# Retention and two gated layers: first two weight units in quarters, weight steps by tables, product order at the ends

## Chip, core and metric

The kernel runs on one core of a Trainium2 chip. The metric is device time in microseconds (us). Its engines, as the profile names them: TensorE (PE; PEld are its weight loads), VectorE (DVE), ScalarE (ACT), GpSimd (POOL) and SyncE (SP), which issues most of the loads.

## The reference

Attention with decay (retention) over 2 batches, 8 heads, 768 positions and head size 64, then two feed-forward layers over its 1536 rows of 512:

```python
state = gamma[None, :, None, None] * state + np.einsum('bhd,bhe->bhde', k[:, :, t], v[:, :, t])
y[:, :, t] = scale * np.einsum('bhd,bhde->bhe', q[:, :, t], state)
...
x = (x @ w_a) * (x @ w_b) @ w_out          # 512 -> 1536 -> 512
h = x @ w_in                               # 512 -> 2048
x = (h * (1.0 / (1.0 + np.exp(-1.702 * h)))) @ w_out
```

## The kernel before

**Retention.** Twelve blocks `n` of 128 positions. Each has on PE scores (`ps_sc`), the state update (`ps_kv`, not for the last block of a sequence), and `ps_av` from the masked scores `a` and from the state; scores of block n+1 are issued at the start of block n. DVE masks the scores (L207), POOL scales q and v, ACT copies the state and casts results. Inputs come as `qv` and `kk`, 512 KB each (`kk` of a sequence's last block 256 KB), four buffers each: a load waits until the block four before has let its buffer go.

**Numbers.** Matmuls run on pairs of high and low parts (`a1h`, `a1l` and so on): ACT casts the high part, DVE subtracts for the low one (L66). The layers' products use a scheme with seven products in place of eight: each *job* (12 in layer 1, 8 in layer 2) has products named 1 to 7, of 12 matmuls each. Products 1, 2, 3 use direct weights `wd`, the others sums of them, `wt`. Product (j, i) is product i of job j. Behind product 1, ACT copies its bank x into bank y (L648), on which 6, 5 and 3 go on; behind 6 and 5 it copies y to `u` (L654, L656). 7 and 4 build a set w, which takes a bank of the same pool as x. Results are added or multiplied into `g` on DVE (L72, L75) or POOL.

**Weights** are stored in 64 bits and converted on the chip, in *units* of 1 MiB (`wraw`, two buffers): load (SP, two halves); *carry* (two ACT operations, L403 and L404); *bits* (two DVE, L409, L410), *sign* (DVE, L416), *add* (DVE, L422: adds what the low words carry). Then the `wd` cast on ACT (L434) and its low part on DVE, four *sums* on DVE (`tt`), and the `wt` cast and low part. `w_stream` is a generator of these steps; each `w_step` takes one, and `w_need` takes steps until the weights wanted are there.

**Order.** All engines run in the order in which the code is written. In retention, `EARLY_STEPS` says which steps of units 0 and 1 stand in which block; units 0 and 1 are loaded whole at the end of blocks 2 and 6 (`W_LOADS`). In `up`, behind each product one function of the list `later` (left-over splits of the retention results, or of layer 2's input sums `s12`, `s34`) or one weight step is taken, in layer 2 one of each. `down` multiplies with `w_out`: blocks of four 128-wide chunks of `g` (split to `ghl`), four quarters q each; `tick` takes one weight step behind each product there. Behind layer 1's down stage its sums become layer 2's operands.

Of the kernel before, what the change touches and what calls it, by code (L numbers as in the profile page):

```python
# [40 lines left out]
def retention_moe_kernel(  # L41
# [324 lines left out]
    wraw, wt, wtt = {}, {}, {}  # L366
    whl, w_half = {}, {}
    nxt = {"dma": 0}
    w_pools = {"d": [[wd, 2]], "t": []}
    w_where = {}  # L370
    more = {}
# [1 line left out]
    def w_room(kind):  # L373
        return sum(p[1] for p in w_pools[kind])

    def w_dma():
        i = nxt["dma"]
        if i >= len(units):
            return
        nxt["dma"] += 1  # L380
        what, ph, *rest = units[i]
        w = w1 if ph == 1 else w2
        t = rawp.tile([P, W, 2], I32, tag="wraw", name="wraw", bufs=2)
        v = t.rearrange("p a b -> p (a b)")
        if what == "d":
            for k, f in enumerate(rest):
                nc.sync.dma_start(out=v[:, k * W:k * W + W], in_=w[f][:, 3 - ph, :].bitcast(I32))
        else:

            p, m = rest  # L390
            nc.sync.dma_start(out=v[:, DM:DM + W], in_=w[2 * p][:, m, :].bitcast(I32))
            nc.sync.dma_start(
                out=v.rearrange("p (a b) -> p a b", a=4)[:, 0:4:3],
                in_=w[2 * p + 1][:, m, :].bitcast(I32).rearrange("p (a b) -> p a b", a=2),
            )
        wraw[i] = t
# [35 lines left out]
    def w_hi(kind, key, src):  # L432
        t = w_tile(kind, key)
        nc.scalar.copy(t[:, 0, 0:src.shape[-1]], src)  # L434
        w_half[kind, key] = t
# [34 lines left out]
        at = DM * (d_unit(f).index(f[1], 1) - 1)  # L470
        return whl["t", d_unit(f)][:, part, at:at + DM]

    EARLY = 1
    EARLY_STEPS = {5: [("carry", 0)], 6: [("bits", 0)], 7: [("sign", 0)], 8: [("add", 0)], 9: [("d", 0)], 10: [("sums", 0), ("carry", 1)], 12: [("second", 0)]}
    W_LOADS, LATER = (2, 6), (9,11)

    def w_stream():

        for i, u in enumerate(units):
            if i < EARLY:  # L480
                continue
            w_bits(i)
            yield
            w_sign(i)
            yield
            w_add(i)
            yield
            if u[0] == "j":
                while not w_room("d"):
                    yield  # L490
                w_hi(*w_direct(i))
                w_sums(i)
                yield
                w_lo(*w_direct(i))
                while not w_room("t"):
                    yield
                w_hi(*w_second(i))
                w_carry(i + 1)
                yield
                w_lo(*w_second(i))  # L500
                wt.pop(i)
                wtt.pop(i)
                yield
            else:
                while not w_room("t"):
                    yield
                it = "t", u[1:], wt.pop(i)
                w_hi(*it)
                w_carry(i + 1)
                yield  # L510
                w_lo(*it)
                yield
# [13 lines left out]

    POOL_LO = {}

    def w_early(n):

        for step, i in EARLY_STEPS.get(n, ()):
            if step == "sums":
                w_sums(i)
            elif step == "second":
                w_hi(*w_second(i))
                w_lo(*w_second(i))
                wt.pop(i)
                wtt.pop(i)
            elif step == "d":
                w_hi(*w_direct(i))  # L540
                w_lo(*w_direct(i))
            else:
                {"carry": w_carry, "bits": w_bits, "sign": w_sign, "add": w_add}[step](i)

# [5 lines left out]
    def retention_done():  # L550

        retention.close()
        kw = dict(reuse_waits="tile")
# [26 lines left out]
    class Job:  # L580
# [54 lines left out]
        def step(self, i):  # L635
# [34 lines left out]
                    return [(self.ph, 2 * self.p), (self.ph, 2 * self.p + 1)]  # L670
            return []

    def up_order(ph, n):
        if ph == 1:
            yield from ((0, 1), (0, 2), (0, 6), (0, 5), (0, 7), (0, 3), (1, 1), (0, 4), (1, 6), (1, 2), (1, 5))
        else:
            yield from ((0, 1), (1, 1), (0, 2), (1, 2), (0, 6), (1, 6), (0, 5), (1, 5), (0, 7), (0, 3), (2, 1), (0, 4))
            yield from ((2, 2), (1, 7), (2, 6), (1, 3), (2, 5), (1, 4))
# [3 lines left out]
        yield from ((j, 1), (j - 1, 7), (j, 2), (j - 1, 3), (j, 6), (j - 1, 4), (j, 5), (j, 7), (j, 3), (j, 4))  # L682

    ghl = {}
    saved = {}
# [35 lines left out]
    def up(ph):  # L721
        jobs = [Job(k) for k in jobs_of(ph)]
        n = len(jobs)
        n_chunks = (C1, C2)[ph - 1]
        order = [*up_order(ph, n)]
        todo = []
        for at, (j, i) in enumerate(order):
            ready = jobs[j].step(i)
            finish()
            for _ in range(2 if ph == 1 and 0 < at < 3 else 1):  # L730
                if later:
                    later.pop(0)()
            if not later or ph == 2:
                w_step()
            for f in todo:
                g_save(f)
            todo = [f for f in ready if f[1] < n_chunks - 6]
            if j == n - 1:

                room["big"] += {2: 2, 5: 2, 3: 2, 4: 1}.get(i, 0)  # L740
                g_next(ph, 4)
        assert not todo and not later

    def down(ph):
# [136 lines left out]
    with tc.manual_schedule():  # L881
        for t in state:
            nc.vector.memset(t, 0.0)
        att_constants()
        for n in range(RAWBUFS):
            att_load(n, "qv")
            att_load(n, "kk")
        ps = ps_att.tile([P, NP, P], F32, tag="av", name="ps_warm", bufs=3)
        warm(ps, WARM)
        att_v(0)  # L890
        att_load(RAWBUFS, "qv")
        att_vdec([1])
        nc.vector.tensor_scalar(
            out=causal, in0=causal, scalar1=0.0, scalar2=1.0, op0=ALU.is_gt, op1=ALU.mult
        )
        att_scores(0)
        att_q(1)
        att_qdec(2)
        warm(ps, 8, WARM)
        for n in range(NBLK):  # L900
            if n > 0:
                att_scores(n + 1)
            att_s_hi(n - 2)
            if n == 0:
                att_v(1)
                att_q(2)
                att_vdec(range(2, SEQ))
            else:
                att_q(n + 2)
                att_v(n + 1)  # L910
            att_load(n + 1 + RAWBUFS, "qv")
            att_kv(n)
            att_x_vector(n - 1)
            att_s_lo(n - 2)
            att_load(n + RAWBUFS, "kk")
            if n == 0:
                att_qdec(0)
            for c in ((3,), (4, 5))[n] if n < 2 else ():
                att_qdec(c)
            w_early(n)  # L920
# [6 lines left out]
            if n in W_LOADS:  # L927
                w_dma()
            if n in LATER:
                later.pop(0)()  # L930
# [11 lines left out]
        later[:0] = [lambda: (w_early(NBLK), att_s_hi(NBLK - 1), att_s_lo(NBLK - 1))]  # L942
        layer(1)
        layer(2)

# [65 lines left out]
```

## Time and profile before

| | |
|---|---|
| median of 3 runs (lowest, highest) | 608.9 us (608.0, 609.19) |
| profiled execution: time, span | 611.0 us, 609.2 us |
| mean granted clock of PE | 0.988 of 2.4 GHz |
| PE busy | 579.2 us, 95% |
| DVE, ACT, POOL busy | 420.9, 295.9, 66.0 us |
| DMA | 76.9 MB, 126 GB/s in the mean |

Busy shares are means over stages. Where time can go shows in the idle time of PE and in what released it: a row of the timeline carries in brackets the idle time before an instruction and its releaser.

### The profile page before, as it was taken

Reading aid. Unit: us, or ns where it says so; the run is one execution under the profiler, and the core shown is the slowest. Engines: PE = TensorE matmul, PEld = TensorE weight load, DVE = VectorE, ACT = ScalarE, POOL = GpSimd, SP = SyncE. Lnnn points to the kernel's source line nnn. Section 1 sums busy time; section 2 is a strip of 40 time slices with the busy share of each in tenths; the row PEclk is TensorE's granted clock in tenths of the full one; section 3 lists DMA queues with packets and bytes.
Section 4 is the critical chain, followed back from the end, with each engine's and each line's share of the span. In section 5 each row is a group of like instructions: output and inputs, shape, how many; then the busy total and the mean of one; then the engine's idle time right before and its main releaser. Section 6 shows DMA issues by size and latency. Waiting matters only on the chain.

```text
span 609.2 us, 8443 instructions
## 1 busy us (share of the span) xinstructions
PE 579.2 (95%) x3448; PEld 528.7 (87%) x3448; DVE 420.9 (69%) x478; ACT 295.9 (49%) x366; POOL 66.0 (11%) x145
## 2 busy tenths in 40 slices
PE   8979789999999999899999988999999999999997
PEld 8868679999999999788887877999998888888885
DVE  3669968788878866656688797776645646776422
ACT  3746543654554647337133475676658547070100
POOL 6844002030302030200000000000000000000000
PEclk9979989999999999999999998999999999999999
DMA  8982023424262222351503002564422443430022
GB/s 310 308 318 92 12 90 106 173 76 168 74 238 70 69 70 70 114 231 57 185 21 118 1 24 83 214 265 175 173 70 69 170 176 130 165 118 39 0 104 104
DMA packets 24263, 76.90 MB, mean 126 GB/s; under 512 B 2336, under 2 KB 2464, under 8 KB 24224
## 3 DMA queue, kind: packets, MB, share of 16 engines
q1 hardware_dynamic: 23648, 75.77, 35.2%
q8 instruction: 27, 0.44, 0.3%
q10 hardware_dynamic: 576, 0.59, 0.3%
q14 instruction: 12, 0.10, 0.1%
HBM read 60.62 MB, written 15.73 MB: 125 GB/s over the span
## 4 chain that ended last, share of the span: by engine, by line
PE 75%; DVE 14%; ACT 4%; DMA 4%; issue 3%; POOL 0%; ACTq 0%; DVEq 0%
PE ps L605 36%; PE ps L835 34%; DMA kk<-in_att_dram 3%; PE ps_sc L198 2%; DVE tt L69 2%; DVE wt L422 1%; DVE sum L72 1%; PE ps_av L244 1%; DVE wt L416 1%; DVE s34l L66 1%; DVE sum L69 1%; PE ps_kv L226 1%; ACT wraw L404 1%; ACT wt L403 1%; DMA causal<-in_cmask_dram 1%
## 5 line engine op out<-in xcount | busy, mean ns | idle before, releaser
L835 PE MATMUL ps<-wt,ghl 128*128 128x512 f32 x576 | 131.1, 389 | 0.8 <-DVE sum L72 0.8
L835 PEld LDWEIGHTS ps<-wt,ghl 128*128 128x128 f32 x576 | 108.0, 188 | 23.6 <-DVE sum L72 1.2
L835 PE MATMUL ps<-ghl,wt 128*128 128x512 f32 x432 | 98.7, 390 | 2.7 <-DVE g L75 2.1
L835 PEld LDWEIGHTS ps<-ghl,wt 128*128 128x128 f32 x432 | 80.9, 188 | 20.2 <-DVE g L75 2.6
L605 PE MATMUL ps<-a1h,wd 128*128 128x384 f32 x320 | 89.2, 341 | 7.8 <-DVE wd L66 3.0
L605 PE MATMUL ps<-s12h,wt 128*128 128x384 f32 x320 | 87.4, 335 | 1.0 <-ACT u L654 1.0
L66 DVE TENSOR_TENSOR ghl<-g,ghl 128x1536 fp32r<-128x1536 f32 x28 | 50.8, 1816 | 48.0 <-ACT ghl L272 47.9
L272 ACT CAST ghl<-g 128x1536 fp32r<-128x1536 f32 x28 | 41.0, 1481 | 58.1 <-PE ps L835 50.6
L605 PEld LDWEIGHTS ps<-a1h,wd 128*128 128x128 f32 x320 | 59.3, 192 | 10.0 <-DVE wd L66 4.0
L72 DVE TENSOR_TENSOR sum<-ps,sum 128x512 f32<-128x512 f32 (+1 forms) x41 | 36.9, 932 | 39.7 <-PE ps L835 39.6
L605 PEld LDWEIGHTS ps<-s12h,wt 128*128 128x128 f32 x320 | 58.3, 188 | 1.6 <-ACT u L654 1.4
L605 PE MATMUL ps<-s12l,wt 128*128 128x384 f32 x160 | 53.7, 336 | 1.5 <-DVE s12l L66 1.5
L605 PE MATMUL ps<-a1l,wd 128*128 128x384 f32 x160 | 54.2, 339 | 0.0
L72 DVE TENSOR_TENSOR u<-ps,u 128x768 f32<-128x768 f32 x28 | 26.8, 956 | 33.8 <-PE ps L605 32.1
L605 PE MATMUL ps<-s34h,wd 128*128 128x384 f32 x160 | 45.2, 344 | 3.1 <-ACT u L656 2.1
L75 POOL TENSOR_TENSOR g<-g,u 128x768 f32<-128x768 f32 x12 | 29.2, 2431 | 172.5 <-DVE u L72 113.3
L605 PE MATMUL ps<-a,wt 128*128 128x384 f32 x240 | 44.8, 334 | 0.0
L422 DVE CUSTOM_DVE_ANT_0 wt<-wraw,wt 128x2048 uint16<-128x2048 uint16 x34 | 43.3, 1273 | 1.4
L605 PE MATMUL ps<-s34h,wt 128*128 128x384 f32 x160 | 43.8, 334 | 0.0
L416 DVE SCALAR_TENSOR_TENSOR wt<-wraw,wt 128x1024 int32<-128x1024 int32 x34 | 41.5, 1221 | 0.6
L605 PEld LDWEIGHTS ps<-a,wt 128*128 128x128 f32 x240 | 41.9, 188 | 0.0
L403 ACT ACTIVATE wt<-wraw 128x1024 f32<-128x1024 f32 x34 | 38.8, 1141 | 2.6 <-DMA wraw<-in_w_dram 2.6
(92 smaller groups left out, 817.0 us busy)
## 6 DMA issues: line engine op xcount, KB each, us to landing
wraw<-in_w_dram SPq DMA_DIRECT2D x68, 512.0 KB, 4.6
spilled<-g SPq DMA_DIRECT2D x16, 768.0 KB, 4.8
g<-spilled SPq DMA_DIRECT2D x16, 768.0 KB, 6.4
qv<-in_att_dram SPq DMA_DIRECT2D x11, 512.0 KB, 8.1
kk<-in_att_dram SPq DMA_DIRECT2D x9, 512.0 KB, 8.9
out_dram<-sum SPq DMA_DIRECT2D x3, 512.0 KB, 2.8
out_dram<-sum SPq DMA_DIRECT2D x6, 256.0 KB, 2.4
kk<-in_att_dram SPq DMA_DIRECT2D x3, 256.0 KB, 5.6
```

Of the source, the lines that this page charges most:

```text
L66: engine.tensor_tensor(out=lo, in0=src, in1=hi.bitcast(F32), op=ALU.subtract)
L69: nc.vector.tensor_tensor(out=o, in0=a, in1=b, op=ALU.subtract)
L72: nc.vector.tensor_tensor(out=o, in0=a, in1=b, op=ALU.add)
L75: engine.tensor_tensor(out=o, in0=a, in1=b, op=ALU.mult)
L198: nc.tensor.matmul(ps[:, h2, p * P:(p + 1) * P], kk_t[n][rows, 0, p * P:(p + 1) * P], q[rows, p, :], start=(p == 0), stop=True, skip_group ...
L226: nc.tensor.matmul(ps[64 * h2:64 * h2 + 64, p, :], kk_t[n][:, 1, h * D:(h + 1) * D], v_t[n][:, h, :], start=(c == 0 and p == 0), stop=True ...
L272: nc.scalar.copy(hi, src)
L403: nc.scalar.activation(out=wt[i], in_=high.bitcast(F32), func=ACTF.Abs)
L416: nc.vector.scalar_tensor_tensor(out=ti, in0=wraw[i][:, :, 1], scalar=-0x40000000, in1=ti, op0=ALU.bitwise_and, op1=ALU.bitwise_or)
L422: nc.vector.tensor_tensor(out=ti, in0=ti, in1=wraw.pop(i)[:, :, 0], op=ALU.add)
L605: nc.tensor.matmul(ps[b][:, 0] if len(ps) > 1 else ps[0][:, b], w_operand(self.key, i, wp)[:, kc * P:(kc + 1) * P], r.operand(i, xp)[:, kc ...
L835: nc.tensor.matmul(banks[n], l, r, start=(f == block[0] and i == 0), stop=(f == block[-1] and i == 2), skip_group_check=True,)
```

## The change

- `w_dma` can load a quarter (256 KB) of a job's unit. `BLOCK` says for block n and place 0, 1 or 2 in it which step stands there: unit 0 is loaded in quarters in blocks 0 to 2 and converted in blocks 4 to 7, unit 1 loaded in quarters in blocks 3 to 9, its carry stands in block 9 and its bits in block 10; unit 2 is loaded at the end. During retention `w_add` no longer loads.
- The direct operand of unit 0 (`d`, block 6) now stands ahead of its add (block 7): this one operand leaves out what the low words add to the last bits.
- `UP` gives by layer and product number what is taken behind that product (`w` a weight step, `l` a function of `later`); `DOWN` gives the number of weight steps at some ticks. Without an entry it is as before.
- `HEAD` and `TAIL` write the product order at both ends of `up`. In layer 1, (0,4) now stands ahead of (1,1), and at the end (10,7), (11,1), (10,3), (11,2), (11,6), (10,4), (11,7), (11,5) take the place of (11,1), (10,7), (11,2), (10,3), (11,6), (10,4), (11,5), (11,7). In layer 2, three pairs change places.

```diff
-    def w_dma():
+    def w_dma(part=None):
...
+        if not part:
+            wraw[i] = rawp.tile([P, W, 2], I32, tag="wraw", name="wraw", bufs=2)
...
+                f, half = ((0, 0), (0, 1), (1, 0), (1, 1))[part]
+                to = ((1, 2), (0, 3))[f][half]
+                nc.sync.dma_start(
+                    out=v[:, to * DM:to * DM + DM],
+                    in_=w[2 * p + f][:, m, half * (DM // 2):(half + 1) * (DM // 2)].bitcast(I32),
+                )
+        if part is None or part == 3:
+            nxt["dma"] += 1
...
-        w_dma()
+        if not retaining:
+            w_dma()
...
-    EARLY_STEPS = {5: [("carry", 0)], 6: [("bits", 0)], 7: [("sign", 0)], 8: [("add", 0)], 9: [("d", 0)], 10: [("sums", 0), ("carry", 1)], 12: [("second", 0)]}
-    W_LOADS, LATER = (2, 6), (9,11)
...
+        (4, 1): (('carry', 0), ('bits', 0)),
+        (5, 0): (('sign', 0),),
+        (6, 0): (('d', 0), ('load', 1)),
...
+        (1, 8): ('', 'wwwl'),
+        (1, 10): ('', ''),
+        (1, 13): ('', 'ww'),
...
+        (2, 2): ('', 'wlw'),
...
+        for step, i in BLOCK.get((n, place), ()):
+            begun.add((steps[step], i))
+            steps[step](i)
...
+        1: ((-1, 7), (0, 1), (-1, 3), (0, 2), (0, 6), (-1, 4), (0, 7), (0, 5), (0, 3), (0, 4)),
...
+            aside(before)
             ready = jobs[j].step(i)
             finish()
-            for _ in range(2 if ph == 1 and 0 < at < 3 else 1):
-                if later:
-                    later.pop(0)()
-            if not later or ph == 2:
-                w_step()
+            aside(after)
...
-            w_step()
+            for _ in range(DOWN.get((ph, ticks[0]), 1)):
+                w_step()
+            ticks[0] += 1
```

How the change moves rows at three places. First SP's loads in blocks 0 to 3, as a piece of the difference; the first row is the keys of block 4, and `wraw` is a weight unit:

```order
 L136 DMA kk<-in_att_dram 128x1024
+L402 DMA wraw<-in_w_dram 128x512 x2
 L130 DMA qv<-in_att_dram 128x2x512
 L136 DMA kk<-in_att_dram 128x512
+L402 DMA wraw<-in_w_dram 128x512
 L130 DMA qv<-in_att_dram 128x2x512
 L136 DMA kk<-in_att_dram 128x1024
-L391 DMA wraw<-in_w_dram 128x1024
-L392 DMA wraw<-in_w_dram 128x2x512
+L402 DMA wraw<-in_w_dram 128x512
```

The two halves of unit 0 (L391, L392) stood behind the keys of block 6 (the row of 128x1024 ahead of them); now two quarters stand behind those of block 4 and one behind each of blocks 5 and 6.

Next DVE in blocks 4 to 8 (L207 masks one block's scores, `wt` and `wd` are unit 0). Before:

```order
L409 TENSOR_SCALAR wt<-wt 128x1024
L410 TENSOR_SCALAR wt<-wt 128x1024
L207 TENSOR_TENSOR a<-ps_sc,causal 128x1024
L66 TENSOR_TENSOR a1l<-ps_av,a1h 128x4x128
L66 TENSOR_TENSOR s12l<-ps_av,s12h 128x4x128
L416 SCALAR_TENSOR_TENSOR wt<-wraw,wt 128x1024
L207 TENSOR_TENSOR a<-ps_sc,causal 128x1024
L69 TENSOR_TENSOR x<-x,ps_av 128x256
L72 TENSOR_TENSOR ps_av<-ps_av,x 128x256
L69 TENSOR_TENSOR ps_av<-ps_av,x 128x256
L69 TENSOR_TENSOR x<-x,ps_av 128x256
L422 ISA wt<-wraw,wt 128x2048
```

Now:

```order
L420 TENSOR_SCALAR wt<-wt 128x1024
L421 TENSOR_SCALAR wt<-wt 128x1024
L207 TENSOR_TENSOR a<-ps_sc,causal 128x1024
L427 SCALAR_TENSOR_TENSOR wt<-wraw,wt 128x1024
L66 TENSOR_TENSOR a1l<-ps_av,a1h 128x4x128
L66 TENSOR_TENSOR s12l<-ps_av,s12h 128x4x128
L207 TENSOR_TENSOR a<-ps_sc,causal 128x1024
L66 TENSOR_TENSOR wd<-wt,wd 128x768
L69 TENSOR_TENSOR x<-x,ps_av 128x256
```

Bits stood ahead of the mask of block 7; they now stand ahead of that of block 6, and sign and the low part of `wd` follow within the next two masks.

Last ACT at the head of layer 2, where job 0 and job 1 run their products 6, 5, 7 and 3 (`u` copies) and the casts of `s34` are taken from `later`. Before:

```order
L272 CAST s34h<-sum 128x768
L434 CAST wd<-wt 128x768
L654 COPY u<-ps 128x768
L272 CAST s34h<-sum 128x768
L434 CAST wt<-tt 128x1024
L403 ACTIVATE wt<-wraw 128x1024
L404 ACTIVATE wraw<-wraw 128x1024
L656 COPY u<-ps 128x768
L272 CAST s34h<-sum 128x768
L656 COPY u<-ps 128x768
L272 CAST s34h<-sum 128x768
```

Now:

```order
L272 CAST s34h<-sum 128x768
L728 COPY u<-ps 128x768
L272 CAST s34h<-sum 128x768
L446 CAST wd<-wt 128x768
L272 CAST s34h<-sum 128x768 x2
L730 COPY u<-ps 128x768
L446 CAST wt<-tt 128x1024
L414 ACTIVATE wt<-wraw 128x1024
L415 ACTIVATE wraw<-wraw 128x1024
L730 COPY u<-ps 128x768
```

The wt cast and the two carries behind it (L403 and L404, now L414 and L415) stood ahead of both last casts of `s34` and of both L656 copies; they now stand behind the casts and behind the first of those copies.

## Rows read from the trace of the kernel before

**Rows 1.** Windows: length, PE, PEld, DVE, ACT, POOL busy (instructions), clock, DMA share, GB/s.

```profile
25.00:38.00 13.00, 8.36 (x129) 7.46 (x128) 5.28 (x9) 5.50 (x10) 8.13 (x14) 0.89 0.95 349
38.00:62.00 24.00, 22.00 (x334) 19.64 (x332) 22.58 (x37) 15.44 (x32) 9.83 (x13) 0.92 0.45 147
62.00:77.00 15.00, 11.87 (x63) 11.00 (x64) 14.38 (x25) 8.80 (x17) 0.00 (x0) 0.97 0.13 34
77.00:91.00 14.00, 11.90 (x60) 11.26 (x59) 9.14 (x12) 5.86 (x7) 0.00 (x0) 0.91 0.19 63
108.00:199.00 91.00, 90.84 (x524) 90.52 (x523) 77.02 (x91) 47.44 (x55) 14.85 (x6) 1.00 0.37 127
```

**Rows 2.** Timeline of the loads: start us, us, engine, line, what [idle before, releaser].

```profile
22.88 0.43 SPq L391 DMA_DIRECT2D wraw<-in_w_dram  x1
...
24.46 0.66 SPq L136 DMA_DIRECT2D kk<-in_att_dram  x1
...
33.08 1.12 ACT L403 ACTIVATE wt<-wraw 128x1024 f32<-128x1024 f32 x1 [2.59 <-DMA wraw<-in_w_dram]
...
35.76 0.59 PE L198 MATMUL ps_sc<-q,kk 64*128 64x128 f32 x2 [3.79 <-DMA kk<-in_att_dram]
```

**Rows 3.** The same view as rows 1 for two stretches of the loads.

```profile
9.00:18.00 9.00, 8.83 (x136) 7.96 (x136) 4.91 (x5) 7.95 (x22) 6.63 (x13) 1.00 1.04 400
22.00:27.00 5.00, 4.89 (x98) 4.56 (x98) 3.68 (x5) 2.89 (x8) 3.85 (x7) 1.00 0.86 233
```

**Rows 4.** The page's DMA issues: count, KB each, median us to landing.

```profile
kk<-in_att_dram SPq DMA_DIRECT2D x9, 512.0 KB, 8.9
...
kk<-in_att_dram SPq DMA_DIRECT2D x3, 256.0 KB, 5.6
```

**Rows 5.** Timeline of PE: two blocks' scores; product (2,1) released, and its successor.

```profile
44.68 1.16 PE L198 MATMUL ps_sc<-q,kk 64*128 64x128 f32 x16
...
48.13 1.16 PE L198 MATMUL ps_sc<-q,kk 64*128 64x128 f32 x16
...
91.03 0.61 PE L605 MATMUL ps<-a1h,wd 128*128 128x384 f32 x2 [0.51 <-DVE wd L66]
...
92.90 0.34 PE L605 MATMUL ps<-s34h,wt 128*128 128x384 f32 x1
```

**Rows 6.** Waits of PE: releaser, us in total, times, longest.

```profile
PE ps_sc L198 <- DMA kk<-in_att_dram: 4.8, 3, 3.8
PE ps L605 <- DVE wd L66: 3.0, 3, 1.5
PE ps L605 <- ACT wd L434: 2.9, 2, 1.6
PE ps L605 <- ACT u L656: 2.1, 2, 1.4
PE ps L835 <- DVE g L75: 2.1, 1, 2.1
...
PE ps L835 <- DVE sum L72: 1.4, 2, 0.8
```

**Rows 7.** Timeline of PE: first product of layer 2, and product (2,1) there.

```profile
346.80 0.33 PE L605 MATMUL ps<-a1h,wd 128*128 128x384 f32 x1
...
375.86 0.53 PE L605 MATMUL ps<-a1h,wd 128*128 128x384 f32 x1
```

**Rows 8.** Timeline of DVE at the head of layer 2.

```profile
355.66 1.22 DVE L66 TENSOR_TENSOR wt<-tt,wt 128x1024 fp32r<-128x1024 f32 x1
356.79 0.95 DVE L66 TENSOR_TENSOR s12l<-sum,s12h 128x768 fp32r<-128x768 f32 x1
```

**Rows 9.** Timeline of ACT in the tail of layer 1's up stage.

```profile
195.69 1.05 ACT L434 CAST wt<-tt 128x1024 fp32r<-128x1024 f32 x1 [2.25 <-DVE tt L69]
...
198.74 0.77 ACT L656 COPY u<-ps 128x768 f32<-128x768 f32 x1
```

**Rows 10.** The page's costliest groups: an addition from PSUM.

```profile
L72 DVE TENSOR_TENSOR u<-ps,u 128x768 f32<-128x768 f32 x28 | 26.8, 956 | 33.8 <-PE ps L605 32.1
```

More of the change, by code (lines that the diff above doesn't have):

```diff
@@ L471, in d_operand @@
         return whl["t", d_unit(f)][:, part, at:at + DM]
-    EARLY = 1
-    EARLY_STEPS = {5: [("carry", 0)], 6: [("bits", 0)], 7: [("sign", 0)], 8: [("add", 0)], 9: [("d", 0)], 10: [("sums", 0), ("carry", 1)], 12: [("second", 0)]}
-    W_LOADS, LATER = (2, 6), (9,11)
+    begun = set()
+    BLOCK = {
+        (0, 1): (('load', 0),),
+        (1, 0): (('load', 1),),
+        (1, 1): (('load', 2),),
+        (2, 2): (('load', 3),),
+        (3, 1): (('load', 0),),
+        (4, 1): (('carry', 0), ('bits', 0)),
+        (5, 0): (('sign', 0),),
+        (6, 0): (('d', 0), ('load', 1)),
+        (7, 1): (('add', 0), ('later', 0)),
+        (8, 1): (('load', 2),),
+        (9, 0): (('load', 3),),
+        (9, 2): (('carry', 1),),
+        (10, 0): (('later', 0), ('bits', 1)),
+        (11, 2): (('load', None), ('sums', 0)),
+    }
@@ new lines, in retention_moe_kernel @@
+    UP = {
+        (1, 2): ('', 'lll'),
+        (1, 3): ('', 'ww'),
+        (1, 7): ('', 'ww'),
+        (1, 8): ('', 'wwwl'),
+        (1, 10): ('', ''),
+        (1, 13): ('', 'ww'),
+        (1, 14): ('', ''),
+        (1, 16): ('', 'ww'),
+        (1, 18): ('', ''),
+        (1, 19): ('', 'll'),
+        (1, 20): ('', 'ww'),
+        (1, 22): ('', 'ww'),
+        (1, 23): ('', ''),
+        (1, 26): ('', ''),
+        (1, 28): ('', ''),
+        (1, 30): ('', 'ww'),
+        (1, 31): ('', 'ww'),
+        (1, 32): ('', ''),
+        (1, 49): ('', ''),
+        (1, 51): ('', ''),
+        (1, 79): ('', 'ww'),
+        (2, 0): ('', 'l'),
+        (2, 1): ('', 'l'),
+        (2, 2): ('', 'wlw'),
+        (2, 5): ('', 'lwll'),
+        (2, 7): ('', 'l'),
+        (2, 22): ('', ''),
+        (2, 25): ('', 'lwlw'),
+        (2, 27): ('', 'l'),
+        (2, 34): ('', 'l'),
+        (2, 38): ('', 'l'),
+    }
@@ L477, in w_stream @@
+    DOWN = {
+        (1, 14): 0,
+        (1, 16): 0,
+        (1, 29): 0,
+        (1, 30): 2,
+        (1, 32): 0,
+        (1, 41): 0,
+        (1, 42): 0,
+        (1, 43): 0,
+        (2, 16): 0,
+    }
     def w_stream():
         for i, u in enumerate(units):
-            if i < EARLY:
+            if i == 0:
                 continue
[L482 to L487, printed above, removed]
+            for step in (w_bits, w_sign, w_add):
+                if (step, i) not in begun:
+                    step(i)
+                    yield
@@ L527, in retention_moe_kernel, with w_second_whole, w_direct_whole, at_block @@
     POOL_LO = {}
[L529 to L543, printed above, removed]
+    def w_second_whole(i):
+        w_hi(*w_second(i))
+        w_lo(*w_second(i))
+        wt.pop(i)
+        wtt.pop(i)
+    def w_direct_whole(i):
+        w_hi(*w_direct(i))
+        w_lo(*w_direct(i))
+    def at_block(n, place):
+        steps = {
+            "carry": w_carry, "bits": w_bits, "sign": w_sign, "add": w_add, "d": w_direct_whole,
+            "sums": w_sums, "load": w_dma, "later": lambda _: later.pop(0)(),
+        }
+        for step, i in BLOCK.get((n, place), ()):
+            begun.add((steps[step], i))
+            steps[step](i)
     chunk = {}
@@ L681, in up_order @@
         j = n - 1
-        yield from ((j, 1), (j - 1, 7), (j, 2), (j - 1, 3), (j, 6), (j - 1, 4), (j, 5), (j, 7), (j, 3), (j, 4))
+        yield from ((j + k, i) for k, i in TAIL[ph])
     ghl = {}
@@ L726, in up, with aside @@
         todo = []
+        def aside(what):
+            for c in what:
+                if c == "w":
+                    w_step()
+                elif later:
+                    later.pop(0)()
         for at, (j, i) in enumerate(order):
+            before, after = UP.get((ph, at), ("", "lw" if ph == 2 else "l" if later else "w"))
+            aside(before)
             ready = jobs[j].step(i)
             finish()
-            for _ in range(2 if ph == 1 and 0 < at < 3 else 1):
-                if later:
-                    later.pop(0)()
-            if not later or ph == 2:
-                w_step()
+            aside(after)
             for f in todo:
@@ L926, in retention_moe_kernel @@
             att_x(n)
[L927 to L930, printed above, removed]
+            at_block(n, 2)
         nc.tensor.matmul(
@@ L941, in retention_moe_kernel @@
         att_x_vector(NBLK - 1)
-        later[:0] = [lambda: (w_early(NBLK), att_s_hi(NBLK - 1), att_s_lo(NBLK - 1))]
+        later[:0] = [lambda: (w_second_whole(0), att_s_hi(NBLK - 1), att_s_lo(NBLK - 1))]
         layer(1)
```

37 lines of the change are left out of this document (22 added, 15 removed).

## Prediction

> **What bounds the kernel now.** I read the windows first, then the waits of TensorE (PE), then the timeline where they fall. In the middle of layer 1 (108 to 199 us) PE is busy 90.8 of 91 us at full clock, 0.174 us per matmul, so a product of twelve takes 2.08 us [rows 1]; nothing but fewer or faster matmuls would help there, and the change brings neither. What it can win lies where PE stands idle or ran at half clock: between 25 and 91 us, and at the seams between stages.
>
> From 25 to 38 us the loads are late. SyncE issues the two halves of weight unit 0 at 22.88 us, just ahead of the keys of block 7 (24.46). ScalarE waits 2.59 us for the unit and gets it at 33.08; PE waits 3.79 us for the keys, until 35.76 (4.8 us for keys in all [rows 6]), and behind that idle time the granted clock falls to the lower of its two levels, 1.2 of 2.4 GHz, for a while: 0.89 in the mean of the window to 38 us, 0.92 to 62 [rows 1, 2]. The loads ran at 400 GB/s from 9 to 18 us, but at 233 from 22 to 27 [rows 3]. From 38 on VectorE (DVE) takes over: busy 22.6 of 24 us and 14.4 of the next 15 [rows 1], and PE waits five times for direct operands (wd) that come from its conversions or ScalarE's: 3.0 and 2.9 us in all [rows 6]. Behind 91 us the waits are single ones: for u copies 2.1 us in two, for g 2.1, for sum 1.4 in two [rows 6], and a cluster at the head of layer 2, where ten products that need 20.8 us take 29.1, from 346.80 to 375.86 [rows 7].
>
> **Term 1: blocks 6 to 11 and layer 1 up to product (2,1).** The quarters of unit 0 enter the queue earlier: two behind the keys of block 4, near 12.5 us, where loads ran at full rate and then stopped for lack of free buffers. From 18 us until the keys of block 7 have landed the queue must move 3.9 MB: five whole att loads of 0.52 MB, one of half that, and the four quarters of 0.26. At 400 GB/s that ends at 27.8 us, at 233 at 34.9; I take 320, between them, and so 30 us, since the quarters lie apart; unit 0 is then complete near 27 us (2.9 MB), not at 33. Block 7's scores are due at about 31, so the 3.8 us go, and with them the half clock that followed.
>
> Now DVE is the limit. From 25 to 91 us it does 5.3 + 22.6 + 14.4 + 9.1 = 51.4 us of work [rows 1], at whose end the low half of wd for unit 2 releases (2,1) at 91.03 [rows 5]. The change moves this work and removes none of it, except that one g product of 0.95 us falls behind that point: 50.4 us. It starts 0.7 us into the stretch and will still idle some 0.5 to 3 us (for unit 0, for scores, for PE's results): the operand is ready at 25 + 0.7 + 50.4 + 0.5 to 3 = 76.6 to 79.1, not 91.0. Since (2,1) ended 1.9 us after its release (92.90 [rows 5]), it ends at 78.5 to 81.0. PE alone would need, from 28 us, some 6.3 blocks at 3.45 us (44.68 to 48.13 [rows 5]) and twelve products at 2.08, so 46.7 us, to 74.8; the 4 to 6 us between are waits that stay: for score tiles of blocks 8 and 9 (1 to 2 us), for the copies behind (0,1) that free its banks (2), the low half of wt for (0,6) (0.7), and a new one: (1,6) now follows (1,1) at once, so the copy of y (0.8 us, like the u copy of 0.77 [rows 9]) lies bare, where (0,4) covered it. I take 79.7: **13.2 us gained** (11.9 to 14.4).
>
> **Term 2: product (3,1)**, which waited 1.5 us for wd, the longest of those three [rows 6]. With unit 2 twelve microseconds sooner, unit 3 has its wd three products early: **1.5**.
>
> **Term 3: the tail of layer 1's up stage.** One of the u waits is 0.7 us at 199.6, because the cast of wt and both carries (195.69 to 198.74, 3.05 us) stand ahead of the u copy on ScalarE [rows 9]. In the new order that copy comes first there: **0.7**. At the step into the down stage PE waited 2.1 us for a g product [rows 6] that stood behind two ghl splits on DVE; it now stands behind one sign step, while product (11,4) of 2.08 us runs: **2.1**. Against that, (11,7) now follows (10,4) directly and its set takes the bank that (10,4)'s addition has still to read; an addition lasts 0.96 us [rows 10], and with the handover that **costs 1.1** where (11,5) lay between before.
>
> **Term 4: the last block of down 1.** The sum of the second quarter waited behind a weight addition, and PE for it, 0.6 of the 1.4 us [rows 6]; it now stands ahead of it: **0.6**.
>
> **Term 5: the head of layer 2.** Of the 8.2 us lost there [rows 7], the clearest part is on DVE: the second low half s12l came after a wt conversion of 1.13 us (355.66 to 356.79 [rows 8]), and so each later one behind a step. On ScalarE wd, then wt and two carries (again about 3 us) stood ahead of the u copies and the last s34 casts. In the new order two s12l stand together, the casts and first copies come ahead of wt. Laid out with these durations, (0,6) still waits 0.4 us for s12l, (0,5) 0.35, (0,3) 0.5 for its u copy and 0.45 for s34l, and restarts add 0.6: 2.3 lost, and the half clock that ended the cluster does not come. **5.9** (4 to 6.4). At the tail of layer 2 ScalarE's order round the last u copy is unchanged: its 1.4 us stay.
>
> **Cover.** The table doubles the weight steps behind some ten products and skips others. Where that is free, the following product covers it (2.08 us against two steps of about 1.2); where a result on DVE comes behind it and a bank is wanted, it costs up to 1. I take 1.5 off, from 0 to 3. Eight quarter loads in place of four halves cost SyncE four more issues, hidden while it waits for buffers anyway; if a quarter held it up, the q and v of a later block would be late by as much.
>
> Sum: 13.2 + 1.5 + 0.7 + 2.1 - 1.1 + 0.6 + 5.9 - 1.5 = 21.4 us. The profiled execution has a span of 609.2 and a time of 611.0, 2.1 over the median of the runs; both fall by the same, so the median goes from 608.9 to 587.5.
>
> **A rule weighed.** Loads of keys of 256 KB landed in 5.6 us and those of 512 KB in 8.9 [rows 4], so here smaller loads were not worse off than larger ones beside them. The Trainium skill ("DMA: Bandwidth & Descriptors", Rules for kernel authors) asks for at least 1 MiB per DMA, and its fit (Anatomy of one DMA) gives each transfer about 2.0 us that do not shrink with size. By that the two additional transfers ahead of block 7's keys would cost up to 4 us if nothing overlapped, an estimate from that page, and the case would become rival A; the overlap of eight loads in flight is why I don't expect it.
>
> **Rivals.** A: the quarters move at the low rate, and the keys of block 7 land at 34.9. Then the idle PE and the half clock behind it stay, and of term 1 there is left 0.9 us at the keys, 1.0 ahead of block 6, the 4.4 of the waits for wd that term 2 doesn't count [rows 6] and some 1 us of half clock round 77 (0.91 in that window [rows 1]): 7 of the 13.2, and the time is **593.7**. For it speaks the 233 GB/s beside unit 0; against it the 400 before.
>
> B: new waits. DVE is busy 77 of 91 us in the up loop [rows 1]; if the shifted steps leave 0.4 us at each of the 20 jobs, 8 us go: **595**. Against it: the loop lost nothing before, in nearly the same order.
>
> C, slower: in every job the u copy falls behind wt and the two carries, as at 199.6. At 0.7 us for each of 20 jobs that is 14 and still a gain; it decides from 21.4/20 = 1.07 us, and at 1.5 the time is **617**. Two of the jobs showed such a wait before, so a phase that hits all is remote.
>
> D: DVE idles less than I allow and nothing new appears: 14.4 for term 1, 6.4 for term 5, no deduction, so **584.3**.
>
> **Chances.** The forecast (585 to 591) 0.60, A 0.15, B 0.13, D 0.08, C or worse 0.02, no change 0.02. A measurement tells this kernel from no change at about 0.2%, 1.2 us. Faster 0.96, same 0.02, slower 0.02. The range goes from D down to 583.5 and up through the middles of A and B to 595; the forecast's own is 585 to 591.
>
> **What will show it.** Block 7's scores at 30 to 32 us with no idle time ahead of them and full clock until 60; unit 0's carry on ScalarE at 27 to 29; (2,1) done near 80; no wait for wd; some 1 us ahead of (11,7); about 2 us of waits at the head of layer 2 instead of 8. Wrong it would be if the keys of block 7 still came after 34, if the clock fell again between 50 and 60 while (0,2) and (0,6) wait, or if waits for u or y copies appear all through the up stages.

## The result and the profile after

| | before | after |
|---|---|---|
| median (lowest, highest of 4 runs) | 608.45 us (607.27, 609.19) | 588.99 us (588.86, 590.43) |
| profiled execution: time, span | 611.0, 609.2 us | 590.43, 588.6 us |
| mean granted clock of PE | 0.988 | 1.000 |

The ratio is 0.9687, 95% interval 0.9665 to 0.971; 587.5 was forecast. First the windows of the changed kernel (length, PE, PEld, DVE, ACT, POOL busy, clock, DMA share, GB/s), which answer to [rows 1]:

```profile
25.00:38.00 13.00, 9.90 (x170) 8.86 (x172) 9.28 (x14) 8.01 (x17) 11.48 (x16) 1.00 0.97 350
38.00:62.00 24.00, 21.46 (x310) 18.74 (x306) 23.57 (x41) 16.68 (x36) 9.13 (x12) 1.00 0.38 121
62.00:77.00 15.00, 13.99 (x79) 13.68 (x80) 14.11 (x22) 8.00 (x12) 0.00 (x0) 1.00 0.21 71
77.00:91.00 14.00, 14.00 (x83) 14.00 (x82) 11.99 (x15) 6.09 (x7) 2.71 (x1) 1.00 0.22 75
```

PE's granted clock is 1.00 throughout (2.4 GHz, the upper of its two levels), where from 25 to 91 us it was 0.92 in the mean, and from 77 to 91 us PE is busy all of 14 us where it was 11.9. VectorE does 9.28 us in the first stretch in place of 5.28. PE's waits, which answer to [rows 6]:

```profile
PE ps L679 <- ACT u L730: 2.7, 3, 1.4
PE ps_av L244 <- DVE a1l L66: 1.6, 1, 1.6
PE ps L679 <- ACT ps L722: 1.6, 2, 0.9
...
PE ps_sc L198 <- POOL q L75: 1.5, 1, 1.5
PE ps_av L244 <- DVE a L207: 1.1, 1, 1.1
PE ps L923 <- DVE sum L72: 0.8, 1, 0.8
...
PE ps L679 <- DVE s12l L66: 0.3, 1, 0.3
```

No row is left for keys, for wd or for the g product at down 1; sum stands once in place of twice. New are waits inside the blocks (a1l, q). To see where the time came from, five places of PE's timeline: the product behind (2,1), the new wait of layer 1's tail, the first product of layer 2, (2,1) there, and the last stretch of the kernel:

```profile
83.86 0.33 PE L679 MATMUL ps<-s34h,wt 128*128 128x384 f32 x1
...
230.56 0.44 PE L679 MATMUL ps<-s34h,wd 128*128 128x384 f32 x1 [0.94 <-ACT u L730]
...
332.80 0.33 PE L679 MATMUL ps<-a1h,wd 128*128 128x384 f32 x1
...
355.68 0.33 PE L679 MATMUL ps<-a1h,wd 128*128 128x384 f32 x1
...
579.17 5.76 PE L923 MATMUL ps<-wt,ghl 128*128 128x512 f32 x24 [0.78 <-DVE sum L72]
```

The first is 92.90 before [rows 5], so 9.04 us are won there. At the first product of layer 2 it is 346.80 - 332.80 = 14.00, so 4.96 more between; its head takes 22.88 in place of 29.06 us [rows 7], 6.18 more. The last stretch began at 599.70 before: 20.53 in all. The medians lie 19.46 apart, since the profiled execution of before was 2.6 over its median and this one 1.4.

In the blocks it went otherwise than forecast:

```profile
30.28 1.19 ACT L414 ACTIVATE wt<-wraw 128x1024 f32<-128x1024 f32 x1 [2.74 <-DMA kk<-in_att_dram]
...
31.50 0.69 DVE L420 TENSOR_SCALAR wt<-wt 128x1024 f32<-128x1024 f32 x1 [2.57 <-ACT wt L414]
...
31.63 2.29 POOL L75 TENSOR_TENSOR q<-qv,qdec 128x256 f32<-128x256 f32 x2 [0.50 <-PE ps_av L255]
...
32.22 1.10 DVE L421 TENSOR_SCALAR wt<-wt 128x1024 int32<-128x1024 int32 x1
...
32.91 1.16 PE L198 MATMUL ps_sc<-q,kk 64*128 64x128 f32 x16 [1.45 <-POOL q L75]
...
33.24 1.21 DVE L207 TENSOR_TENSOR a<-ps_sc,causal 128x1024 f32<-128x1024 f32 x1
...
36.02 1.42 POOL L75 TENSOR_TENSOR q<-qv,qdec 128x256 f32<-128x256 f32 x2
...
36.33 1.09 PE L244 MATMUL ps_av<-a,v 128*64 128x128 f32 x16 [1.65 <-DVE a1l L66]
```

ScalarE stands 2.74 us until unit 0 is there, at 30.28 (its last quarter landed 7.8 us after its issue at 22.39; the releaser printed is another load of that moment). VectorE waits 2.57 for that carry, with the mask of block 6 (33.24) behind the two bits. Block 7's scores start at 32.91: the row names q, but the q of that block was done at 29.98, and the keys landed 8.3 us after their issue at 24.44, at 32.74. That landing differs from one execution to the next: with the same blocks it lies between 30.8 us (e8_tails below) and 32.7, and in a second profile of this kernel (after2 below) at 31.2, where PE doesn't wait for the keys but 1.46 us for a1l. Then PE waits 1.65 for the low half a1l, which stood behind bits, mask and sign.

### The profile page after: what moved, and what is told of

It reads as the page before. It is cut to its first block, busy times and chain, and to the rows that moved or that the text cites. A ratio compares the mean times of both kernels' runs of the same rounds, so it can differ in the third digit from the quotient of the medians.

```text
span 588.6 us, 8444 instructions
## 1 busy us (share of the span) xinstructions
PE 572.1 (97%) x3448; PEld 523.9 (89%) x3448; DVE 418.8 (71%) x478; ACT 296.2 (50%) x366; POOL 69.2 (12%) x145
## 4 chain that ended last, share of the span: by engine, by line
PE 85%; DVE 9%; DMA 3%; ACT 1%; issue 1%; POOL 0%; ACTq 0%; DVEq 0%
PE ps L679 45%; PE ps L923 38%; DMA kk<-in_att_dram 2%; DVE a L207 1%; DVE s12l L66 1%; DVE sum L69 1%; DMA causal<-in_cmask_dram 1%; DVE sum L72 1%; DVE s34l L66 1%; PE ps_sc L198 1%; DVE a L66 1%; DVE x L69 1%; PE ps_av L244 0%; DVE wt L433 0%; DVE wt L66 0%
## 5 line engine op out<-in xcount | busy, mean ns | idle before, releaser
L679 PE MATMUL ps<-a1h,wd 128*128 128x384 f32 x320 | 87.4, 335 | 0.7 <-ACT ps L722 0.7
L66 DVE TENSOR_TENSOR ghl<-g,ghl 128x1536 fp32r<-128x1536 f32 x28 | 49.5, 1767 | 47.5 <-ACT ghl L272 47.5
L433 DVE CUSTOM_DVE_ANT_0 wt<-wraw,wt 128x2048 uint16<-128x2048 uint16 x34 | 45.4, 1334 | 2.0
L414 ACT ACTIVATE wt<-wraw 128x1024 f32<-128x1024 f32 x34 | 38.9, 1145 | 2.7 <-DMA kk<-in_att_dram 2.7
```

Of the source, the lines that this page charges most:

```text
L66: engine.tensor_tensor(out=lo, in0=src, in1=hi.bitcast(F32), op=ALU.subtract)
L414: nc.scalar.activation(out=wt[i], in_=high.bitcast(F32), func=ACTF.Abs)
L679: nc.tensor.matmul(ps[b][:, 0] if len(ps) > 1 else ps[0][:, b], w_operand(self.key, i, wp)[:, kc * P:(kc + 1) * P], r.operand(i, xp)[:, kc ...
```

## Experiments

Ratios are to the kernel before, run beside them.

**The blocks alone.** The changed `BLOCK` with product order, `UP` and `DOWN` of before:

```diff
...
-            before, after = UP.get((ph, at), ...)
...
+            for _ in range(2 if ph == 1 and 0 < at < 3 else 1):
+                if later:
+                    later.pop(0)()
+            if not later or ph == 2:
+                w_step()
```

> Only the retention part of the change: unit 0 and the first quarter loads as in the changed kernel, steps in the blocks as there; product order and weight steps behind products as before the change. My theory (the gain up to product (2,1) of layer 1 comes from the earlier conversions, nothing of it from the tables): (2,1) ends within 1 us of 83.9 us and the waits of layer 2's head and at the step into down 1 are back, so 609.2 less 9 is a span near 600 and a median near 599 to 600. Rival (the tables for layer 1 are needed for it, since DVE's steps behind the first products decide when wd of units 1 and 2 are ready): (2,1) ends at 87 or later, median 602 to 605.

604.09 us, 0.9939 (0.9914 to 0.9963), where before was 607.66: the rival, though the product behind (2,1) comes at 86.22, short of its 87. PE's timeline, from the first product of layer 1 on:

```profile
54.47 0.44 PE L679 MATMUL ps<-a1h,wd 128*128 128x384 f32 x1
...
70.50 0.62 PE L679 MATMUL ps<-a1h,wd 128*128 128x384 f32 x2 [1.17 <-DVE wd L66]
...
82.48 0.44 PE L679 MATMUL ps<-a1h,wd 128*128 128x384 f32 x1 [1.62 <-ACT wd L446]
...
83.61 0.62 PE L679 MATMUL ps<-a1h,wd 128*128 128x384 f32 x2 [0.52 <-DVE wd L66]
...
86.22 0.52 PE L679 MATMUL ps<-s34h,wt 128*128 128x384 f32 x1
...
101.50 0.61 PE L679 MATMUL ps<-a1h,wd 128*128 128x384 f32 x2 [1.49 <-DVE wd L66]
```

The waits for wd are back. At (2,1) they are 1.62 with 0.52 and at (3,1) 1.49, to 0.01 us those that the kernel before has there; only at (1,1) are they shorter, 1.17 where before has 1.30 with 1.02. Yet unit 0 was converted blocks sooner, and the first product started 4 us earlier. The window in which those of (2,1) fall shows why, with VectorE's row ahead of it:

```profile
74.65 0.96 DVE L72 TENSOR_TENSOR g<-ps,u 128x768 f32<-128x768 f32 x1 [2.67 <-PE ps L679]
...
77.00:91.00 14.00, 11.86 (x58) 11.23 (x57) 8.66 (x12) 6.05 (x7) 0.61 (x1) 0.88 0.23 75
```

VectorE is busy for 8.66 of 14 us, so it is not the limit; PE's clock falls to 0.88 in the mean. Before it began the bits of unit 2, at 75.53, it stood idle for 2.67 us until 74.65, for a result of PE that it adds first. What is late is the release of the steps. A unit is six weight steps and a job seven products; without the tables each product of layer 1 is followed by one step, and behind the first products `later` takes the places. So the stream starts behind and gains one step per job.

**The tables alone.** Loads and steps of the blocks as before, orders and tables as changed:

```diff
...
+        (2, 2): (('load', None),),
+        (5, 1): (('carry', 0),),
+        (6, 1): (('bits', 0),),
+        (6, 2): (('load', None),),
...
-        (1, 3): ('', 'ww'),
+        (1, 3): ('', 'www'),
```

> The opposite of e1_blocks_only: loads and steps of the retention part as before the change, product order and tables as changed (one more weight step behind the fourth product, for the bits of unit 1 that are no longer done in the blocks). My theory after e1_blocks_only (the waits for wd come from the pace of the weight steps, not from the landing of the units): PE waits for the keys of block 7 as before, until near 35.7, and the first product of layer 1 starts near 58.6, but the waits for wd of 3.0 and 2.9 us are nearly gone (at most 1.5 in all), (2,1) ends near 87.5, and the time is 3 to 5 us over after2, 592 to 594. Rival (units 1 and 2 must be early for the tables to work): the waits for wd stay, (2,1) ends near 92 and the time is 597 to 600.

591.57 us, 0.9725 (0.9699 to 0.975); the changed kernel on the same chip (called after2) gave 589.6, 0.9682 (0.9655 to 0.9709).

> The changed kernel itself, beside the three below on one chip, as their reference: 589.0 within 0.7.

```profile
33.78 1.19 PE L198 MATMUL ps_sc<-q,kk 64*128 64x128 f32 x16 [2.14 <-DMA kk<-in_att_dram]
...
55.30 0.44 PE L675 MATMUL ps<-a1h,wd 128*128 128x384 f32 x1
...
84.73 0.33 PE L675 MATMUL ps<-s34h,wt 128*128 128x384 f32 x1
```

PE still waits 2.14 us for the keys, but for wd not at all, and the product behind (2,1) starts at 84.73: 0.87 after the changed kernel. My theory on wd held and erred only on the size: the time is below its 592 to 594, since the keys came at 33.8 here and not at 35.7. So the blocks alone win 3.6 us, the tables and orders alone 17.3, both 19.2. Tables and orders were not tried apart; but round (2,1) and (3,1) the order of products is that of before, so there it is the tables that took the waits away.

**Layer 2 as before**, its order and its table (the entries of `UP` with 2 ahead left out):

> The changed kernel with layer 2's product order at both ends and layer 2's table of steps as before the change. My theory: the head of layer 2 alone carried 6.2 us (22.9 us for ten products in place of 29.1), so the time is 589.0 + 6.2 = 595.2 and nothing else moves. Rival: half of it came from weight units that were ready sooner because layer 1 ended with the stream further on: then the head loses only some 3 us, 592.

595.91 us, 0.980 (0.9774 to 0.9825): 6.9 us over the changed kernel by the ratios (0.9687 and 0.980 of 608), where 6.18 was expected. In its own trace the head takes 27.84 us (332.19 to 360.03), 4.96 over the changed kernel's 22.88, at a clock of 1.00; the kernel before takes 29.06 at a mean clock of 0.95, so some 1.2 of the 6.18 is clock. The profiled execution is the fastest of the four (594.82); the others had a mean clock of 0.994 to 0.997.

**Carry and bits one block later.**

```diff
-        (4, 1): (('carry', 0), ('bits', 0)),
-        (5, 0): (('sign', 0),),
-        (6, 0): (('d', 0), ('load', 1)),
+        (5, 1): (('carry', 0), ('bits', 0)),
+        (6, 0): (('load', 1), ('sign', 0)),
+        (7, 0): (('d', 0),),
```

> The changed kernel with carry and bits of unit 0 one block later (behind the last low halves of block 5 rather than of block 4), sign and wd also one block later. My theory: since unit 0 lands at 30.2 us, the two bits stood in front of the mask of block 6 and VectorE waited 2.57 us with that mask behind it; now the mask and two low halves fall into that idle time, VectorE's unbroken chain from 31.5 us is shorter by about 2.4 us, the first product of layer 1 starts near 53.6 instead of 55.8 and the time falls by 1.5 to 2.4, to 586.6 to 587.5. Rival (keys of block 7, which land at 32.7, set the end of retention whatever VectorE does): the first product stays within 0.5 us of 55.8 and the time within 0.5 us of 589.0.

589.32 us, 0.9694 (0.967 to 0.9718): no change, my theory fell.

```profile
33.13 1.16 PE L198 MATMUL ps_sc<-q,kk 64*128 64x128 f32 x16 [1.68 <-DMA kk<-in_att_dram]
...
36.45 1.16 PE L198 MATMUL ps_sc<-q,kk 64*128 64x128 f32 x16 [0.66 <-DMA kk<-in_att_dram]
...
54.87 0.44 PE L679 MATMUL ps<-a1h,wd 128*128 128x384 f32 x1
```

The wait for a1l is gone, and PE waits for the keys of blocks 7 and 8 instead, 1.68 and 0.66. In this execution VectorE's stall and the late keys lay side by side. None of its five runs was under 589.02.

**Unit 1 later, unit 0 in halves.** One kernel moves the first quarter of unit 1 from behind the keys of block 7 to two blocks later:

```diff
-        (3, 1): (('load', 0),),
...
+        (5, 1): (('load', 0),),
```

> The changed kernel with the first quarter of unit 1 two blocks later (behind the keys of block 9 instead of block 7). My theory (loads in flight share the bandwidth, so what is issued behind the keys of block 7 delays them): they land 0.3 to 0.7 us earlier than 32.74; but since VectorE's chain starts with unit 0, which was issued before, the first product moves by less than 0.3 us and the time stays within 0.5 us of 589.0. Rival 1 (loads land in the order of issue): keys of block 7 land within 0.2 us of 32.74. Rival 2 (the keys set the end of retention): the time falls by as much as the keys come earlier, 588.3 to 588.7.

589.64 us, 0.9699 (0.9677 to 0.972).

```profile
32.76 1.16 PE L198 MATMUL ps_sc<-q,kk 64*128 64x128 f32 x16 [1.70 <-DMA kk<-in_att_dram]
...
54.38 0.44 PE L679 MATMUL ps<-a1h,wd 128*128 128x384 f32 x1
```

The keys landed 8.5 us after their issue at 24.16, at 32.66, which by the numbers is rival 1. But with the quarter in its place they land anywhere from 30.8 to 32.7 us, so one execution can't show a gain of 0.3 to 0.7 us or its absence; what stands is that the time didn't fall. The other loads unit 0 as two transfers of 512 KB, behind the keys of blocks 4 and 5:

```diff
...
-        (0, 1): (('load', 0),),
-        (1, 0): (('load', 1),),
-        (1, 1): (('load', 2),),
-        (2, 2): (('load', 3),),
+        (0, 1): (('load', 'h0'),),
+        (1, 1): (('load', 'h1'),),
```

> The changed kernel with unit 0 loaded in two halves of 512 KB, behind the keys of block 4 and block 5, in place of four quarters behind those of blocks 4, 4, 5 and 6. My theory (only the place in the queue matters): the last half, issued 3 us before the last quarter, lands near 28.5 in place of 30.2; the keys of block 6, behind it, come 0.3 to 0.7 us later than 28.2 and PE waits that long for them; the keys of block 7 land at 32.7 as before, so the first product of layer 1 stays between 54 and 56 us and the time within 1 us of 589. Rival (smaller transfers cost more in themselves): with two transfers fewer ahead of them the keys of block 7 land 1 us or more earlier, and the time falls by 1 us or more.

588.91 us, 0.9686 (0.966 to 0.9711), as with quarters.

```profile
28.19 1.16 PE L198 MATMUL ps_sc<-q,kk 64*128 64x128 f32 x16 [0.29 <-DMA kk<-in_att_dram]
...
31.18 1.16 PE L198 MATMUL ps_sc<-q,kk 64*128 64x128 f32 x16
...
53.53 0.44 PE L679 MATMUL ps<-a1h,wd 128*128 128x384 f32 x1
```

Block 6's scores wait 0.29 for keys, as expected, and layer 1 starts at 53.53. Block 7's scores start at 31.18 without a wait: its keys landed 6.6 us after their issue at 24.17, at 30.8, and not at 32.7 as I expected. That is the first half of the rival, but it lies within the scatter of unchanged blocks (30.8 to 32.7), and its second half, 1 us less time, didn't come. With the same blocks, kernels here start layer 1 between 53.4 and 55.9 us in their profiles, so this place moves by 2.5 us from one execution to the next, and smaller differences are not read as the edit's.

**The tail of layer 1.** (11,5) ahead of (11,7) again:

```diff
-        1: (..., (-1, 4), (0, 7), (0, 5), (0, 3), (0, 4)),
+        1: (..., (-1, 4), (0, 5), (0, 7), (0, 3), (0, 4)),
```

> The changed kernel with (11,5) ahead of (11,7) again at the end of layer 1's up stage, all else as changed. My theory after the trace of the changed kernel: the new wait of 0.94 us at 230.56 is at (11,3), which goes on the bank y that ScalarE still copies for (11,5), and (11,7) in between covers it: the wait vanishes with its restart of about 0.25 us, 1.2 us in the distance from the first product of layer 1 to the first of layer 2 (277.0 in the changed kernel, 275.8 here). Theory of the prediction (the price is that (11,7) takes the bank that the addition of (10,4) still reads): the same sign, but then the wait would be ahead of (11,7) in the changed kernel, where none over 0.2 us is. Rival: the g product at the step into down 1 that took 2.1 us before comes back, since (11,7) now ends one product later, and the time is 1 us longer.

591.99 us, 0.9728 (0.9706 to 0.9751): slower, the rival. The 0.94 us are gone, but PE waits 2.46 for g:

```profile
235.61 6.71 PE L923 MATMUL ps<-ghl,wt 128*128 128x512 f32 x22 [2.46 <-DVE g L75]
```

What VectorE and GpSimd did ahead of that:

```profile
230.17 1.75 DVE L66 TENSOR_TENSOR ghl<-g,ghl 128x1536 fp32r<-128x1536 f32 x1
...
230.33 3.28 POOL L75 TENSOR_TENSOR g<-g,u 128x768 f32<-128x768 f32 x1 [18.82 <-DVE u L72]
...
231.84 2.85 DVE L427 SCALAR_TENSOR_TENSOR wt<-wraw,wt 128x1024 int32<-128x1024 int32 x1
...
234.61 0.94 DVE L75 TENSOR_TENSOR g<-g,ps 128x768 f32<-128x768 f32 x1
```

The sign step took 2.85 us, elsewhere 1.22, and ended 1.1 us behind GpSimd's multiplication of g (230.33 + 3.28 = 233.61); the g product that PE waits for stood behind it. Behind the idle time the granted clock was 0.77 in the mean from 236 to 242 us, where the changed kernel's stays at 1.00. Whether GpSimd was the cause I tested with its multiplication on VectorE:

```diff
-                mul(nc.vector if u is None else nc.gpsimd, g, g, src)
+                mul(nc.vector if u is None or (second and self.key == jobs_of(1)[-1]) else nc.gpsimd, g, g, src)
```

> e3_tail1 with one multiplication of g at the end of layer 1 moved from GpSimd to VectorE (where it takes 0.95 us). My theory: in e3_tail1 the sign step took 2.85 us in place of 1.22 because GpSimd's multiplication (3.28 us from 230.33) ran beside it and VectorE had to wait for its end; without it sign takes 1.2, and the g product behind it starts 0.7 us earlier, so PE's wait falls from 2.46 to 1.7 or 1.8. Rival (sign waited there for something else, as for its unit): sign stays at 2.8 and PE's wait grows to 3.4.

592.82 us in one run, with the order of e3_tail1; VectorE's timeline:

```profile
233.76 1.22 DVE L427 SCALAR_TENSOR_TENSOR wt<-wraw,wt 128x1024 int32<-128x1024 int32 x1
234.90 0.95 DVE L75 TENSOR_TENSOR g<-g,ps 128x768 f32<-128x768 f32 x1
```

Sign takes 1.22 again, and PE's wait fell to 1.82, as expected of my theory. Then the repair that moves no work to another engine: the order of e3_tail1 again, with the sign step one product later:

```diff
+        (1, 81): ('', ''),
+        (1, 82): ('', 'ww'),
...
```

> The order of e3_tail1, (11,5) ahead of (11,7), and the sign step that stood ahead of the g product on VectorE taken one product later, together with the add behind it. My theory: (11,7) covers the copy of u, and the g product starts right behind the split of ghl, near 231.9 on e3_tail1's clock, so that neither the 0.94 of the changed kernel nor the 2.46 of e3_tail1 are left; from the first product of layer 1 to the first of layer 2 it takes 275.8 in place of 277.0, and the time is 1.2 below after2. Rival (the g product itself is held up by GpSimd's multiplication that runs beside it, as the sign step was): a wait of 1 us or more for g stays, and the time is that of after2 or above.

588.65 us (587.7 to 588.77), 0.9661 (0.9634 to 0.9687), the lowest of all; after2 had 588.9 to 590.09. No wait of PE is left at either place:

```profile
55.12 0.45 PE L681 MATMUL ps<-a1h,wd 128*128 128x384 f32 x1
...
331.05 0.33 PE L681 MATMUL ps<-a1h,wd 128*128 128x384 f32 x1
```

From the first product of layer 1 to the first of layer 2 it takes 275.93 us; in after2 331.20 - 54.18 = 277.02. The medians differ by 0.95, inside the intervals of the ratios, so that gain stands on the trace.

**The tail of layer 2, the head of layer 1.** With the order of e3_tail1, the step of wt and carries behind (7,5):

```diff
+        (2, 51): ('', 'l'),
+        (2, 52): ('', 'lww'),
...
```

> The changed kernel with the order of e3_tail1, and in layer 2 the weight step that casts wt and runs both carries taken behind product (7,5) instead of behind (6,4), so that the copy of u for (7,5) stands ahead of it on ScalarE. My theory: the 1.43 us that PE waits for that copy at (7,3) go, with 0.25 of restart, beside the 1.2 of e3_tail1: 2.9 us, 586.1. Rival: the unit converted there is needed by the first product of down 2, or the split of g behind it is late, so the wait moves to the first product of down 2 and only the 1.2 are left, 587.8.

591.63 us, 0.9724 (0.9701 to 0.9747), as e3_tail1, whose wait for g stands here too (2.45). The 1.43 are gone, but at 469.61 PE waits 0.85 for a copy of sum on ScalarE:

```profile
467.16 1.49 ACT L272 CAST ghl<-g 128x1536 fp32r<-128x1536 f32 x1 [2.03 <-DMA g<-spilled]
468.55 2.89 ACT L869 COPY sum<-ps 128x1024 f32<-128x1024 f32 x4
```

It stands behind a cast that waits for a `g` that had been stored away and is loaded back; PE came earlier there, but that load did not. Last, on top of e8_tails, (1,1) ahead of (0,4), with wd of unit 1 ahead of its sums:

```diff
+                if i > 1:
+                    w_sums(i)
                 yield
                 w_lo(*w_direct(i))
+                if i == 1:
+                    w_sums(i)
...
```

> e8_tails with (1,1) ahead of (0,4) again in layer 1 and, for unit 1 alone, the low half of wd ahead of the sums on VectorE. My theory: wd of unit 1 is then ready at 69.3 in place of 71.8, (1,1) can start at 70.2 without a wait, and (0,4) covers the copy of its bank y, which PE now waits 0.93 us for at (1,6): 1.2 us less than e8_tails, 584.9. Rival: the sums come later by as much, and so the wt of unit 1, so that (1,6) or (1,5) waits for it by 1 us or more and nothing is won, 586 to 587.

592.35 us, 0.9732 (0.9705 to 0.9759), nothing won. On ScalarE wt now waits for the sums, and the copy of y (L727) stands behind it and both carries:

```profile
71.97 1.05 ACT L446 CAST wt<-tt 128x1024 fp32r<-128x1024 f32 x1 [1.08 <-DVE tt L69]
72.92 1.14 ACT L414 ACTIVATE wt<-wraw 128x1024 f32<-128x1024 f32 x1
...
74.97 0.79 ACT L727 COPY ps<-ps 128x768 f32<-128x768 f32 x1
```

PE waits 1.25 for that copy at (1,6), where it was 0.93.

## Why the prediction was right, and where not

The time, the sign and most places were right; what brings the largest part was not what the prediction credits, and part of the close number is luck. By its terms:

- **Term 1**, 13.2 forecast, 9.04 measured (10.7 in after2's profile, whose product behind (2,1) starts at 82.24). The term credits the early quarters and counts the tables, under "Cover", only as a price. It is rather the other way round. From the first product of layer 1 to the one behind (2,1) it takes 34.28 us before, 31.75 with the blocks alone, 29.43 with the tables and orders alone and 28.05 with both. Of the rest of the 9.04, which lies ahead of that first product, little can be told: it starts at 58.62 in the profile of before, but at 55.30 in the tables-only kernel, whose loads and blocks are the same, so these 3 us lie within the scatter of single executions. In the kernel before, "Now DVE is the limit" holds up to 77 us; from there to 91 its own row shows 9.14 of 14 [rows 1] while PE waits for wd, so there the order of the steps is late and not VectorE's work. In the changed kernel it holds to the end of the stretch, from the bits of unit 0 to the low half of wd for unit 2:

```profile
31.50:81.14 49.64, 43.04 (x467) 39.63 (x468) 48.04 (x75) 32.71 (x60) 15.50 (x18) 1.00 0.40 136
...
80.19 0.95 DVE L66 TENSOR_TENSOR wd<-wt,wd 128x768 fp32r<-128x768 f32 x1
```

VectorE is busy 48.04 of 49.64 us, 97%. Its work from 25 us to there came to 50.85 us, where 50.4 was summed. Mis-sized was its idle time: 56.14 - 50.85 = 5.3 us, where the term has 0.7 and 0.5 to 3. The largest piece is the 2.57 ahead of unit 0's bits: the last quarter landed at 30.2, not near 27. So the operand came at 81.14 and not at 76.6 to 79.1.

PE's own chain, which the term lays beside it, came out as late: the first product of layer 1 at 55.81, where some 51 was needed (79.7 less twelve products and the 3.5 of waits it names behind them). From 28.40 seven blocks remain, not 6.3, and the waits in them are 1.45, 1.65, 1.13 and 0.30, 4.5 us in place of 1 to 2. From there on the sum was right: 28.05 us for twelve products and three waits (0.67, 0.52, 0.93) with what each wait costs beside itself, where 28.5 was summed.

The rate of the loads was no reason: from 18 to 32.9 us they moved 356 GB/s, above the 320 taken. But that is 5.3 MB, not 3.9. By 18 us SyncE had issued 6.0 MB, of which its queue had moved 5.0, so beside the two quarters that the term counts some 0.5 MB of earlier loads, which it leaves out, were still to come; the other 0.8 MB were of loads issued behind those keys, which moved meanwhile. At that rate the two make some 3.6 us, an estimate. Why the keys land 6.4 us after their issue in one execution and 8.4 in another stays open.

- **Term 2**: the 1.5 us are gone, but not for the reason given. With the blocks alone unit 2 was earlier and (3,1) waited 1.49 as before; the tables took it away.
- **Term 3**: 0.7 and 2.1 were right. The price of 1.1 came as 0.94, but at (11,3), which goes on the bank that ScalarE still copies for (11,5), not at (11,7). And gain and price were one edit: without the price (e3_tail1) the 2.1 came back as 2.46, until the step was moved as well.
- **Term 4**: right, that wait for sum is gone.
- **Term 5**: 5.9 forecast, 6.18 measured; of the waits laid out, s12l came as 0.31 (0.4) and the u copy as 0.34 (0.5), the other two not.
- **The deduction** of 1.5 for doubled steps was not needed: between the product behind (2,1) and layer 2 nothing new appears except the 0.94. There 4.96 us were won, where terms 2 to 4 sum to 3.8. So term 1 came out 4.2 us short and the rest some 3 better, and that the two errors offset each other is luck.
- **Rivals**: A's keys at 34.9 didn't come (32.74); in the tables-only kernel, whose scores of block 7 started at 33.78, the time was 2 us over after2. B and C show no row: the wait for u copies is 2.7 us in three, each accounted for above. The rule cited for A (the Trainium skill, "DMA: Bandwidth & Descriptors", Rules for kernel authors) asks for 1 MiB, and no run here loads so much at once; between quarters of 256 KB and halves of 512 KB no difference showed (588.99 and 588.91, ratios 0.9687 and 0.9686). The fixed 2.0 us cited with it are that page's fit for transfers which GpSimd issues, while these loads are SyncE's; no run here measures that part.

## What to carry to other kernels

Before an engine is called the limit, its busy share is read in the very window in which the others wait: 65% there (9.14 of 14 us) meant that the order of the steps, not their work, was late, and tables that release two steps behind some products, with a new order of products, were worth 17.3 us, the earlier loads and conversions alone 3.6. With the changed tables VectorE was busy 97% up to the same product, and only then its work was the limit there. A wait is followed to what stands behind it before its removal is credited: here four of them (VectorE's stall beside late keys, the tails of both layers, the copy of y) only handed over to the next. And before one execution's place is read as an edit's effect, the same place is looked up in other executions of the same code: here the landing of one load moved by 2 us.

## What the runs showed of the hardware

GpSimd and VectorE hold each other up in these rows when all inputs of both lie in SBUF, the memory of the operands. GpSimd's multiplication of 128x768 took 1.84 us at 116.36 of the changed kernel, where VectorE was idle or read from PSUM, the memory of the matmuls' results. It took 3.28 in e3_tail1, where VectorE's split of ghl had started 0.16 us ahead of it, and ended 1.7 us behind that split. The sign step that came next took 2.85 in place of 1.22, and 1.22 with the multiplication away (e12_mul_dve). In the blocks of the changed kernel the same shows at 31.63, where q took 2.29 us and not 1.42 while the second of the bits took 1.10 and not 0.69. The Trainium skill ("SBUF — State Buffer", SBUF: two separate sides) calls the port pair that the two share an exclusive lock, kept by whichever began first for the whole instruction; these rows agree. VectorE's g product, whose second input lies in PSUM, took its usual 0.95 us beside a running multiplication (232.96 in the changed kernel, with GpSimd's from 231.58 to 234.34).
